# Sliding heads of the last two rows of an attention-and-MLP kernel: values as the stationary operand, exponentials as the moving one, row sums spread over 64 partitions

## The chip, the cores and the metric

The kernel runs on one core of a Trainium2 chip. The time is that of one execution on the device, in microseconds (us). The core's engines are named as in the profile: PE is TensorE (matmuls), PEld its weight loads, DVE is VectorE, ACT is ScalarE, POOL is GpSimd, and SP issues DMAs. PSUM is where matmuls write; it has eight banks.

## What is computed

An attention layer with 8 batch rows, 8 heads, 576 positions and head size 64, and behind it a two-layer perceptron. Heads 0 to 3 look at the last 32 positions ("sliding"), heads 4 to 7 at every fourth of the last 128 ("dilated").

```python
scores = scale * np.matmul(q, k.transpose(0, 1, 3, 2))
mask_plain = (rel >= 0) & (rel < 32)
mask_dil = (rel >= 0) & (rel < 128) & (rel % 4 == 0)
attn = np.exp(scores - max);  attn = attn / (sum(attn) + 1e-09)
attn_out = np.matmul(attn, v)
x = attn_out.transpose(0, 2, 1, 3).reshape(B * S, H * D)     # 4608 x 512
h = x @ w_in                                                 # 512 -> 2048
out = (np.maximum(h, 0) ** 2) @ w_out                        # 2048 -> 512
```

## The kernel before

**Layout.** The perceptron wants x with features on partitions: the tile xT has 128 partitions x 4 feature chunks x a ring of 4 x 576 tokens. Chunks 0 and 1 hold the sliding heads (two heads of 64 features each), chunks 2 and 3 the dilated ones. The first product (mm1_tile, matmul at L264) multiplies xT by w_in, ScalarE applies relu (L249), VectorE squares (L253) into g. The second product (mm2, L296) multiplies g by w_out, and store copies the result out. For the last two chunks of 512 tokens the second product has another form (seven_gen, matmuls at L401, sums on VectorE).

**Order.** The order of all instructions on each engine is written out by hand: a generator of perceptron steps stands in a list, and pump(n) takes n steps from it, two matmuls of 512 columns each. For rows 2 to 7 (the loop over b) the perceptron of the row before is pending; attention steps are issued with pump between them: 24 steps first, then the scores (attn_scores, four groups with 4 steps behind each), then the values (attn_values, ten places with 2 steps behind each), then the rest (pump(1000)). Behind row 7 come the two last chunks.

**Scores.** Scores come out transposed, keys on partitions and queries along the free dimension: 128 keys against blocks of 96 queries for the sliding heads (L560), of 72 for the dilated ones (L574). ScalarE takes the exponential into the tile AT (L547), and VectorE multiplies by the mask (L549).

**Values.** The value tile vp holds, for each block of 96 queries and each head, its 128 keys x (64 values and a column of ones). In av_sliding the exponentials are the stationary operand (128 keys x 128 columns) and vp the moving one (65 columns, L615): queries come out on partitions, with 64 values and the sum for each of four heads. normalize takes the reciprocal of the sums, 8 for each partition (L600), and multiplies (L601) into an fp16 tile x. x_sliding then turns that tile with six matmuls against the identity (L644), and ScalarE copies the outcome to xT (L650). The dilated heads go the same way (av_dilated L629, x_dilated L662 and L668). Per row there are three groups of av_sliding (two query blocks each), two of x_sliding, four of av_dilated and two of x_dilated.

**PSUM.** From row 1 on, the perceptron and the turned tiles (except row 1's) take banks 0 to 3 in turn, and all groups of scores and values take two pairs of banks in turn (pairs [2, 3]); so a group of values writes where the group before the last did, and has to wait until normalize has read that one.

**Set-up.** v_ones writes the ones of the value tiles on VectorE (L747 to L750), once for each of two copies of the tiles: at L775 in the start, at L842 before the first perceptron steps in a run. GpSimd casts the values in (L197, L201).

Of the kernel before, what the change touches and what calls it, by code (L numbers as in the profile page):

```python
# [8 lines left out]
FP16 = mybir.dt.float16  # L9
FP32 = mybir.dt.float32  # L10
I16 = mybir.dt.int16
ALU = mybir.AluOpType
ACTF = mybir.ActivationFunctionType
P = 128
# [3 lines left out]
def kernel(  # L18
# [9 lines left out]
    nc = tc.nc  # L28

    B, H, S, D = q.shape  # L30
# [5 lines left out]
    HH = H // 2  # L36
# [5 lines left out]
    HALF = S // 2  # L42
# [3 lines left out]
    QB = 96  # L46
    NB = S // QB
    PADP = P - QB
# [7 lines left out]
    const = ctx.enter_context(tc.tile_pool(name="const", bufs=1))  # L56
# [3 lines left out]
    xp = ctx.enter_context(tc.tile_pool(name="xp", bufs=4))  # L60
# [19 lines left out]
    def pair(dt=FP32):  # L80
        i = pairs[turn["pair"] % len(pairs)]
        turn["pair"] += 1
        b = PS[:, 2 * i : 2 * i + 2, :]
        return b if dt == FP32 else b.bitcast(dt)
# [3 lines left out]
    xT = const.tile([P, NDM, RING], FP16, name="xT")  # L88
# [18 lines left out]
    QKTp = [const.tile([P, 2, 2, PADP + S], FP16, name=f"QKTp{r}") for r in range(2)]  # L107
    QKTd = [const.tile([P, 2, 2, KPAD + S], FP16, name=f"QKTd{r}") for r in range(2)]
    AT = const.tile([P, 8, 640], FP16, name="AT")
    vp = [const.tile([P, NB, HH, D + 2], FP16, name=f"vp{r}") for r in range(2)]  # L110
    vd = [const.tile([P, 2, DIL, HH, D + 2], FP16, name=f"vd{r}") for r in range(2)]
    sv = stg.tile([P, NB, HH, D], FP32, name="sv")
    sd = stg.tile([P, 2, HH, DIL * D], FP32, name="sd")
# [109 lines left out]
    def in_token_order(b, n):  # L223
        o = natp.tile([P, 9, HH, D], FP16, name=f"o{b}", tag="o")
        nc.gpsimd.tensor_copy(o, n.rearrange("p h j d -> p j h d"))  # L225
        return o
# [259 lines left out]
    def pump(n):  # L486
        for _ in range(n):
            while pending:
                try:
                    next(pending[0])  # L490
                    break
                except StopIteration:
                    pending.pop(0)
# [3 lines left out]
    def pt(wide):  # L497
        return pair(FP16)[:, 0, :] if wide else bank(FP16)
# [97 lines left out]
    def normalize(b, what, pav, w):  # L596
        x = xp.tile([QB, 2, HH, D], FP16, name=f"x{b}_{what}", tag="x")
        rcp = xp.tile([QB, 2, HH], FP32, name=f"rcp{b}_{what}", tag="rcp")
        pv = pav[0:w, :, 0 : HH * (D + 2)].rearrange("p i (h d) -> p i h d", d=D + 2)
        nc.vector.reciprocal(rcp[0:w], pv[:, :, :, D])  # L600
        nc.vector.tensor_tensor(  # L601
            out=x[0:w],
            in0=pv[:, :, :, 0:D],
            in1=rcp[0:w].unsqueeze(3).to_broadcast([w, 2, HH, D]),
            op=ALU.mult,
        )
        return x

    def av_sliding(b, mp):
        pav = pair()  # L610
        for i in range(2):
            m = 2 * mp + i
            for h in range(HH):
                off = (h % 2) * 288 + (m % 3) * QB
                nc.tensor.matmul(  # L615
                    pav[:, i, h * (D + 2) : h * (D + 2) + D + 1],
                    AT[:, 2 * (h // 2) + m // 3, off : off + P],
                    vp[b % 2][:, m, h, 0 : D + 1],
                    start=True,
                    stop=True,  # L620
                )
        return normalize(b, f"p{mp}", pav, QB)

    def av_dilated(b, t, a):
        pav = pair()
        for e in range(2):
            for h in range(HH):
                off = e * 288 + h * QD
                nc.tensor.matmul(  # L629
                    pav[:, e, h * (D + 2) : h * (D + 2) + D + 1],  # L630
                    AT[:, 4 + 2 * a + t, off : off + P],
                    vd[b % 2][:, t, 2 * a + e, h, 0 : D + 1],
                    start=True,
                    stop=True,
                )
        return normalize(b, f"d{t}_{a}", pav, QD)

    def x_sliding(b, half, xs, wide):
        px = pt(wide)
        for m3 in range(3):  # L640
            m = 3 * half + m3
            x = xs[m // 2][:, m % 2].rearrange("p h d -> p (h d)")
            for c in range(2):
                nc.tensor.transpose(  # L644
                    px[:, 288 * c + QB * m3 : 288 * c + QB * (m3 + 1)],
                    x[:, P * c : P * (c + 1)],
                    ident[0:QB, 0:QB],
                )
        t0 = (b % 4) * S + 288 * half
        nc.scalar.copy(  # L650
            xT[:, 0:2, t0 : t0 + 288],
            px[:, 0:UW].rearrange("x (c t) -> x c t", c=2),
        )

    def x_dilated(b, t, xs, wide):
        py = pt(wide)
        for a in range(2):
            for e in range(2):
                x = xs[a][:, e].rearrange("p h d -> p (h d)")
                for c in range(2):  # L660
                    o = 288 * c + QD * (2 * a + e)
                    nc.tensor.transpose(  # L662
                        py[:, o : o + QD],
                        x[0:QD, P * c : P * (c + 1)],
                        ident[0:QD, 0:QD],
                    )
        t0 = (b % 4) * S + 288 * t
        nc.scalar.copy(  # L668
            xT[:, 2:4, t0 : t0 + 288].rearrange("x c (i r) -> x c i r", r=DIL),
            py[:, 0:UW].rearrange("x (c r i) -> x c i r", c=2, r=DIL),  # L670
        )
# [8 lines left out]

    def attn_values(b, gap, wide=False):
        xs = []
        for mp in range(3):
            xs.append(av_sliding(b, mp))
            pump(gap)
        x_sliding(b, 0, xs, wide)
        pump(gap)
        ys = [av_dilated(b, 0, 0)]
        pump(gap)
        x_sliding(b, 1, xs, wide)  # L690
        pump(gap)
        ys.append(av_dilated(b, 0, 1))
        pump(gap)
        zs = []
        for a in range(2):
            zs.append(av_dilated(b, 1, a))
            pump(gap)
        x_dilated(b, 0, ys, wide)
        pump(gap)
        x_dilated(b, 1, zs, wide)  # L700
# [43 lines left out]
        )  # L744

    def v_ones(r):
        nc.vector.memset(vp[r][:, :, :, D : D + 1], 1.0)  # L747
        nc.vector.memset(vp[r][0:PADP, 0, :, D : D + 1], 0.0)
        nc.vector.memset(vd[r][:, 1, :, :, D : D + 1], 1.0)
        nc.vector.tensor_scalar(  # L750
            out=vd[r][:, 0, :, :, D],
            in0=relf[:, 0:1].unsqueeze(2).to_broadcast([P, DIL, HH]),
            scalar1=-PADD + 0.5,
            scalar2=None,
            op0=ALU.is_lt,
        )
# [15 lines left out]
    for a in range(2):  # L772
        t_dilated_one(0, nd0, a, 1, tk[:, a, :])
        c_dilated_one(0, a, 1, tk[:, a, :], nc.vector)
    v_ones(0)  # L775
    for a in range(2):
        t_dilated_one(0, nd0, a, 0, tq[:, a, :])
# [49 lines left out]
    xs = [av_sliding(0, mp) for mp in range(2)]  # L827
    x_dilated(0, 0, ys, True)
    x_sliding(0, 0, xs, True)
    pairs[:] = [2, 3]  # L830
    pending.append(mm1_first_gen())
# [8 lines left out]
    x_sliding(0, 1, xs, True)  # L840
    k_pads(1)
    v_ones(1)  # L842
    ns1 = natp.tile([P, HH, 9 * D], FP16, name="ns1", tag="n")
    nd1 = natp.tile([P, 36 * D], FP16, name="nd1", tag="nd")
    for i, src in ((1, k), (0, q)):
        nc.gpsimd.dma_start(
            out=ns1[64 * i : 64 * (i + 1)],
# [19 lines left out]
    o = in_token_order(2, n)  # L867
# [16 lines left out]
    s_dilated(1, 1)  # L884
    pump(4)
    attn_values(1, 1, True)
    pump(1000)
    load_v(2)
# [3 lines left out]
    for b in range(2, B):  # L892
        pending.append(moe_gen(b - 1))
        if b + 1 < B:
            see(QKTp[b % 2][0:1, 0, 0, PADP : PADP + 1])
            n, dd = load_whole_sliding_qk(b + 1), keep_dilated_qk(b + 1)
            o = in_token_order(b + 1, n)
            transpose_dilated(b + 1, dd)
            transpose_sliding(b + 1, keep_sliding_qk(b + 1, o))
        cast_v(b)  # L900
        if b + 1 < B:
            load_v(b + 1)
        if b + 1 < B:
            pump(24)
        else:
            quarters()
            for name in ("T1", "T3", "T2", "T4"):
                for j in range(2):
                    pump(3)
                    sum_w_out(name, j)  # L910
        attn_scores(b, 4)
        attn_values(b, 2)
        pump(1000)
# [33 lines left out]
```

## Time and profile before

| | |
|---|---|
| median of 3 runs (314.5 to 316.2) | 314.87 us |
| the profiled execution | 315.87 us |
| its span, first to last instruction | 313.8 us |
| mean granted TensorE clock | 0.995 |
| busy: PE, DVE, ACT, POOL | 299.6, 181.7, 167.3, 78.0 us |
| values of row 6 | about 212.6 to 225.8 |
| values of row 7 | about 244.9 to 258.1 |

Times in the views count from the span's start. A line such as "L601 ... x24 | 16.5, 686 | 0.8" is a group of instructions: line, engine, operation, output and inputs, shape, count, then busy us, mean ns of one, and the idle time of the engine just before them. The chain is the work that ended last, followed back from the end to what released each step.

### The profile page before, as it was taken

What the parts mean: (1) busy time and instruction counts of PE and PEld (TensorE: products, weight loads), DVE (VectorE), ACT (ScalarE), POOL (GpSimd) and SP (SyncE); (2) the same over time, 40 slices, a digit from 0 to 9 for tenths busy, and PEclk for the clock granted to TensorE, in tenths of its full rate; (3) what the DMA queues carried; (4) which work ended last, traced back from release to release, by engine and by line L of the source; (5) the groups of instructions that cost most, each with busy time, mean ns of one, the idle gap of its engine ahead of it and who ended that gap; (6) DMA issues with size and microseconds to landing.
All of it is one profiled execution on the core that took longest, in us unless ns stands there. A gap on an engine that the chain in (4) does not pass through costs nothing.

```text
span 313.8 us, 6835 instructions
## 1 busy us (share of the span) xinstructions
PE 299.6 (96%) x2724; PEld 183.7 (59%) x2724; DVE 181.7 (58%) x402; ACT 167.3 (53%) x295; POOL 78.0 (25%) x120
## 2 busy tenths in 40 slices
PE   3978999999899999999999999999999999999995
PEld 3647955555455555555579655545554555686584
DVE  6445647736742795396524653475388534854764
ACT  2646856378336753677257724683368336604610
POOL 5483016403523633263340370032000000000000
PEclk9989999999999999999999999999999999999999
DMA  6999989599989999998968992992100110012012
GB/s 118 223 191 214 212 179 216 123 164 256 229 185 202 278 193 188 236 280 172 221 218 193 176 239 75 186 206 101 45 25 1 41 61 36 1 40 96 0 36 100
DMA packets 73951, 46.71 MB, mean 149 GB/s; under 512 B 54528, under 2 KB 68096, under 8 KB 73728
## 3 DMA queue, kind: packets, MB, share of 16 engines
q1 hardware_dynamic: 66384, 32.39, 43.2%
q0 software_dynamic: 7248, 13.63, 24.4%
q8 instruction: 21, 0.34, 0.4%
q10 hardware_dynamic: 288, 0.26, 0.2%
q14 instruction: 10, 0.08, 0.1%
HBM read 39.85 MB, written 16.52 MB: 180 GB/s over the span
## 4 chain that ended last, share of the span: by engine, by line
PE 88%; DMA 7%; POOL 2%; issue 1%; ACT 1%; DVE 0%; POOLq 0%
PE PS L264 39%; PE PS L296 30%; PE PS L401 8%; PE PS L629 3%; DMA wi<-in_moe_w_in_dram 3%; DMA sd<-in_v_dram 2%; DMA n<-in_q_dram 2%; PE PS L615 2%; PE PS L574 1%; PE PS L644 1%; PE PS L560 1%; PE PS L662 1%; ACT AT L547 0%; PE PS L504 0%; PE PS L528 0%
## 5 line engine op out<-in xcount | busy, mean ns | idle before, releaser
L264 PE MATMUL PS<-xT,wi 128*128 128x512 f16 (+3 forms) x704 | 130.3, 343 | 1.8 <-DMA wi<-in_moe_w_in_dram 1.1
L249 ACT ACTIVATE rt<-PS 128x512 f16<-128x512 f32 (+2 forms) x160 | 88.8, 556 | 44.6 <-PE PS L264 40.5
L296 PE MATMUL PS<-wo,g 128*128 128x512 f16 x448 | 112.5, 379 | 0.0
L253 DVE TENSOR_TENSOR g<-rt 128x512 f16<-128x512 f16 (+2 forms) x160 | 69.8, 443 | 72.1 <-ACT rt L249 71.5
L264 PEld LDWEIGHTS <-wi 128*128 128x128 f16 x704 | 78.4, 114 | 46.8 <-DMA wi<-in_moe_w_in_dram 1.2
L296 PEld LDWEIGHTS <-g 128*128 128x128 f16 x448 | 37.3, 97 | 31.4
L547 ACT ACTIVATE AT<-PS 128x576 f16<-128x576 f32 x64 | 38.3, 650 | 8.6 <-PE PS L574 5.7
L306 ACT COPY ot<-PS 128x512 f32<-128x512 f32 x28 | 16.4, 586 | 28.8 <-PE PS L296 28.8
L650 ACT COPY xT<-PS 128x576 f16<-128x576 f16 x16 | 10.2, 639 | 29.4 <-PE PS L644 29.4
L201 POOL CAST vd<-sd 128x512 f16<-128x512 f32 x32 | 20.5, 669 | 14.7 <-DMA sd<-in_v_dram 12.5
L197 POOL CAST vp<-sv 128x512 f16<-128x512 f32 x24 | 16.7, 710 | 27.1 <-DMA sv<-in_v_dram 27.1
L601 DVE TENSOR_TENSOR x_d<-PS,rcp_d 72x512 f16<-72x512 f32 x32 | 22.0, 686 | 1.1
L225 POOL COPY o<-n 128x2304 f16<-128x2304 f16 x6 | 12.6, 2107 | 27.8 <-DMA n<-in_q_dram 27.6
L549 DVE TENSOR_TENSOR AT<-AT,maskd 128x576 f16<-128x576 f16 x28 | 14.6, 539 | 7.0 <-ACT AT L547 5.6
L600 DVE RECIPROCAL rcp_d<-PS 72x8 f32<-72x8 f32 x32 | 6.5, 202 | 20.7 <-PE PS L629 19.6
L629 PEld LDWEIGHTS <-AT 128*128 128x128 f16 x256 | 12.8, 102 | 7.8 <-DVE x_d L601 0.8
L601 DVE TENSOR_TENSOR x_p<-PS,rcp_p 96x512 f16<-96x512 f32 x24 | 16.5, 686 | 0.8
L549 DVE TENSOR_TENSOR AT<-AT,maskp 128x576 f16<-128x576 f16 x28 | 14.3, 524 | 4.0 <-ACT AT L547 2.1
L668 ACT COPY xT<-PS 128x576 f16<-128x576 f16 x16 | 10.2, 640 | 8.8 <-PE PS L662 8.8
L629 PE MATMUL PS<-vd,AT 128*128 128x65 f16 x256 | 14.3, 200 | 0.0
L183 POOL COPY look<-QKTp 1x1 f16<-1x1 f16 x5 | 1.2, 239 | 49.3 <-DMA QKTp<-dp 49.3
L615 PEld LDWEIGHTS <-AT 128*128 128x128 f16 x192 | 9.2, 99 | 6.6 <-issue 1.2
(86 smaller groups left out, 207.9 us busy)
## 6 DMA issues: line engine op xcount, KB each, us to landing
out_dram<-ot SPq DMA_DIRECT2D x27, 256.0 KB, 2.8
sv<-in_v_dram SPq DMA_DIRECT2D x40, 128.0 KB, 4.6
sd<-in_v_dram SPq DMA_DIRECT2D x8, 512.0 KB, 11.4
dp<-o SPq DMA_DIRECT2D x12, 288.0 KB, 3.7
sd<-in_v_dram SPq DMA_DIRECT2D x8, 288.0 KB
wo<-in_moe_w_out_dram POOLq DMA_DIRECT2D x4, 512.0 KB, 13.6
out_dram<-c SPq DMA_DIRECT2D x14, 128.0 KB, 1.8
n<-in_k_dram POOLq DMA_DIRECT2D x6, 288.0 KB, 6.1
```

Source lines behind the costliest of these rows:

```text
L197: nc.gpsimd.tensor_copy(vp[b % 2][:, m : m + 2, :, 0:D], sv[:, m : m + 2, :, :])
L201: nc.gpsimd.tensor_copy(vd[b % 2][:, t, c : c + 2, :, 0:D], sd[:, t, :, D * c : D * (c + 2)].rearrange("p h (c d) -> p c h d", d=D),)
L249: nc.scalar.activation(rt[:, 0:w], ph[:, 0:w], ACTF.Relu)
L253: nc.vector.tensor_mul(g, rt[:, o : o + n], rt[:, o : o + n])
L264: nc.tensor.matmul(ph[:, a:b], w_in_of(dmk, ffc), xT[:, dmk, x : x + b - a], start=(dmk == 0 and a == 0), stop=(dmk == NDM - 1 and b == w),)
L296: nc.tensor.matmul(po, g[:, ffc, o + t * P : o + (t + 1) * P], w_out_of(ffc), start=(ffc == 0), stop=(ffc == NFF - 1),)
L306: nc.scalar.copy(ot, po)
L401: nc.tensor.matmul(po[t], lhs(j)[:, t * P : (t + 1) * P], rhs(j), start=j == 0, stop=j == HF - 1)
L547: nc.scalar.activation(AT[:, u, 0:UW], ps[:, :, 0 : UW // 2], ACTF.Exp, scale=scale)
L549: eng.tensor_mul(AT[:, u, 0:UW], AT[:, u, 0:UW], mask)
L601: nc.vector.tensor_tensor(out=x[0:w], in0=pv[:, :, :, 0:D], in1=rcp[0:w].unsqueeze(3).to_broadcast([w, 2, HH, D]), op=ALU.mult,)
L629: nc.tensor.matmul(pav[:, e, h * (D + 2) : h * (D + 2) + D + 1], AT[:, 4 + 2 * a + t, off : off + P], vd[b % 2][:, t, 2 * a + e, h, 0 : D ...
```

## The change

It touches rows 6 and 7 (b >= B - 2) and the sliding heads alone. The tile vp gets 128 columns for each head in place of 66: 64 values and 64 ones. v_ones fills all 64.

Row 7 (values_of_head): one head at a time. For each of six query blocks, one matmul with a stationary operand of 128 columns, which is the 64 values of the head and 64 ones (for odd heads the ones of the head before stand first), and the exponentials as the moving operand, 96 columns. Values come out with features on partitions and queries along the free dimension, and the other 64 partitions hold the sum of each query, 64 times over. VectorE takes the reciprocal of all these sums (64 partitions x 576) and multiplies the values by it straight into xT.

Row 6 (values_of_two): two heads and half of the queries at a time, in twelve matmuls of 64 stationary columns: values of two heads in one bank, one head on partitions 0 to 63 and one on 64 to 127, and their sums in the other bank. VectorE's reciprocal and product cover 128 partitions x 288.

So in these rows x is not turned, normalize is not used for the sliding heads, and ScalarE doesn't copy them; the four new groups come first, each with a pump behind it, and there are nine such places in place of ten. The dilated heads stay as they are.

```diff
-    vp = [const.tile([P, NB, HH, D + 2], FP16, name=f"vp{r}") for r in range(2)]
+    vp = [const.tile([P, NB, HH, 2 * D], FP16, name=f"vp{r}") for r in range(2)]
...
+    def spread_slots(b, m, h):
+        v_ = vp[b % 2][:, m].rearrange("p h x -> p (h x)")
+        o = 2 * D * h - (D if h % 2 else 0)
+        return v_[:, o : o + 2 * D]
+
+    def exps_of(h, m):
+        off = (h % 2) * 288 + (m % 3) * QB
+        return AT[:, 2 * (h // 2) + m // 3, off : off + QB]
+
+    def values_of_head(b, h):
+        ps = pair()
+        for m in range(NB):
+            o = QB * (m % 3)
+            nc.tensor.matmul(
+                ps[:, m // 3, o : o + QB], spread_slots(b, m, h), exps_of(h, m), start=True, stop=True
+            )
+        e = h % 2
+        mine, other = slice(64 * e, 64 * e + 64), slice(64 - 64 * e, 128 - 64 * e)
+        r = xp.tile([P, 2, HALF], FP32, name=f"r{b}_{h}", tag="r", bufs=1)
+        nc.vector.reciprocal(r[mine], ps[other, :, 0:HALF])
+        t0 = (b % 4) * S
+        nc.vector.tensor_tensor(
+            out=xT[mine, h // 2, t0 : t0 + S].rearrange("p (i t) -> p i t", i=2),
+            in0=ps[mine, :, 0:HALF],
+            in1=r[mine],
+            op=ALU.mult,
+        )
+
+    def values_of_two(b, hp, half):
+        ps = pair()
+        for m3 in range(3):
+            m = 3 * half + m3
+            for i in range(2):
+                for e in range(2):
+                    h = 2 * hp + e
+                    nc.tensor.matmul(
+                        ps[64 * e : 64 * e + 64, i, QB * m3 : QB * (m3 + 1)],
+                        vp[b % 2][:, m, h, D * i : D * (i + 1)],
+                        exps_of(h, m),
+                        start=True,
+                        stop=True,
+                    )
+        r = xp.tile([P, 2, HALF], FP32, name=f"r{b}_{hp}_{half}", tag="r", bufs=1)
+        nc.vector.reciprocal(r[:, 0, :], ps[:, 1, 0:HALF])
+        t0 = (b % 4) * S + HALF * half
+        nc.vector.tensor_tensor(
+            out=xT[:, hp, t0 : t0 + HALF], in0=ps[:, 0, 0:HALF], in1=r[:, 0, :], op=ALU.mult
+        )
...
     def attn_values(b, gap, wide=False):
         xs = []
-        for mp in range(3):
-            xs.append(av_sliding(b, mp))
+        spread = b >= B - 2
+        if spread:
+            for i in range(4):
+                if b == B - 1:
+                    values_of_head(b, i)
+                else:
+                    values_of_two(b, i % 2, i // 2)
+                pump(gap)
+        else:
+            for mp in range(3):
+                xs.append(av_sliding(b, mp))
+                pump(gap)
+            x_sliding(b, 0, xs, wide)
             pump(gap)
-        x_sliding(b, 0, xs, wide)
-        pump(gap)
         ys = [av_dilated(b, 0, 0)]
         pump(gap)
-        x_sliding(b, 1, xs, wide)
-        pump(gap)
+        if not spread:
+            x_sliding(b, 1, xs, wide)
+            pump(gap)
         ys.append(av_dilated(b, 0, 1))
...
     def v_ones(r):
-        nc.vector.memset(vp[r][:, :, :, D : D + 1], 1.0)
-        nc.vector.memset(vp[r][0:PADP, 0, :, D : D + 1], 0.0)
+        nc.vector.memset(vp[r][:, :, :, D : 2 * D], 1.0)
+        nc.vector.memset(vp[r][0:PADP, 0, :, D : 2 * D], 0.0)
```

## The prediction

> **What bounds the kernel now.** I read four views: the page's chain of work, the same chain in order of time, VectorE's timeline beside it, and VectorE's groups by form. The page's chain gives the span to TensorE:
>
> ```profile
> PE 88%; DMA 7%; POOL 2%; issue 1%; ACT 1%; DVE 0%; POOLq 0%
> ```
>
> In order of time, around the values of row 7 (columns: start, us on the chain, what):
>
> ```profile
> 244.93 0.25 PE PS L615 x8
> 245.19 0.86 PE PS L296 x4
> 246.05 0.26 PE PS L615 x8
> ...
> 248.29 0.26 PE PS L644 x6
> 248.54 0.86 PE PS L296 x4
> 249.41 0.25 PE PS L629 x8
> ```
>
> No idle piece stands between them: a group of attention matmuls (0.25 us), four matmuls of the second product (0.86 us), and so on through row 6 (212.6 to 225.8) and row 7 (244.9 to 258.1). An edit gains here only what it takes off TensorE, and anything that makes TensorE wait is lost in full, since the stages behind are as dense. VectorE in the same stretch (columns: start, duration, operation, in brackets idle before):
>
> ```profile
> 245.22 0.20 DVE L600 RECIPROCAL rcp_p<-PS 96x8 f32<-96x8 f32 x1 [0.53 <-PE PS L615]
> 245.46 0.69 DVE L601 TENSOR_TENSOR x_p<-PS,rcp_p 96x512 f16<-96x512 f32 x1
> 246.34 0.20 DVE L600 RECIPROCAL rcp_p<-PS 96x8 f32<-96x8 f32 x1 [0.19 <-PE PS L615]
> 246.58 0.69 DVE L601 TENSOR_TENSOR x_p<-PS,rcp_p 96x512 f16<-96x512 f32 x1
> ```
>
> It needs 0.20 + 0.04 + 0.69 = 0.93 us per group and is offered one each 1.12 us (245.22 to 246.34): 0.19 us are free. These groups write to only two PSUM pairs in turn (pairs [2, 3]), so group n+2 can't start before VectorE is through with group n. That is the wait that ends last if VectorE slows down.
>
> **Removed from TensorE, per row:** three sliding groups (3 x 0.25) and two groups of turning matmuls (2 x 0.26), 1.28 us. ScalarE loses two copies of 0.64 us; it idles up to 3.0 us between such copies in row 7, so that is worth nothing.
>
> **Added on TensorE, row 7:** 4 heads x 6 matmuls of 96 columns from full 128-row weights. L644 is six matmuls of 96 columns: 0.26 us. 4 x 0.26 = 1.04 us, so -0.24 us. **Row 6:** 4 groups of 12 matmuls of 96 columns with 64 weight columns, which the trace before doesn't show. Between 25 ns each (64x64 tiles of L504: 36 of 64 columns in 0.59 us, times 96/64) and 43 ns (L644, nothing overlapped): 1.18 to 2.06 us, -0.1 to +0.8. I take L560's rate, 12 of 96 columns in 0.36 us, as it is the nearest packed row: 4 x 0.36 = 1.44, +0.16 us. Both rows: -0.08 us.
>
> **Added on VectorE: the inverse over everything.** A reciprocal now takes 8 elements per partition; afterwards it takes 576 (row 7, four times) or 288 (row 6, four times). Everything hangs on what one more element costs, and no row shows a long reciprocal. The rows that split a duration into a fixed part and a slope:
>
> ```profile
> L601 DVE TENSOR_TENSOR x_p<-PS,rcp_p 96x512 f16<-96x512 f32 x24 | 16.5, 686 | 0.8
> L600 DVE RECIPROCAL rcp_p<-PS 96x8 f32<-96x8 f32 x24 | 4.8, 202 | 7.1 <-PE PS L615 7.1
> L193 DVE COPY QKTp<-PS 128x576 f16<-128x576 f16 x5 | 3.8, 758 | 4.8 <-PE PS L504 4.8
> L472 DVE TENSOR_TENSOR c<-PS,v 128x256 f32<-128x256 f32 x4 | 1.7, 424 | 1.3 <-PE PS L401 1.3
> L456 DVE TENSOR_TENSOR c<-PS,t 128x512 f32<-128x512 f32 x2 | 1.4, 692 | 0.7 <-PE PS L401 0.7
> L726 DVE CAST relf<-reli 128x96 f32<-128x96 int16 x1 | 0.2, 210 | 0.6 <-POOL reli L710 0.6
> ```
>
> L456 less L472: 268 ns for 256 elements, 1.047 ns each. Taking that slope off, the fixed part of an instruction that reads PSUM is 150 ns (L601), 155 (L193), 156 (L456, L472). The reciprocal reads the same PSUM tile as L601 and takes 203 (its median) for 8 elements, where 153 + 8 would be 161. The missing 42 ns are either fixed, or they belong to the elements. The ends: all fixed, so 1.047 ns each with 195 fixed; or the fixed part is only that of a one-element memset (59 ns, L721), and an element costs 18 ns. I take the fixed part of the rows nearest to it, 153, so (203 - 153) / 8 = **6.25 ns** per element (5.9 to 6.6 over these rows).
>
> Reciprocals: 576 elements 153 + 3600 = 3.75 us, 288 elements 153 + 1800 = 1.95. Products, at L601's fixed part and 1.047 ns: 0.76 and 0.46 us. With the 0.04 us between the two, a head of row 7 costs VectorE 4.55 us and a group of row 6 2.45, where TensorE would bring one each 1.12 and 1.22 (0.26 or 0.36, plus 0.86).
>
> **The wait.** Count from the first group's start. Row 7: VectorE starts at 0.46 (ScalarE's copy starts at 248.58 behind an equal group, six L644, that started at 248.12) and is through with four heads at 0.46 + 4 x 4.55 = 18.66. Dilated group 01 is the sixth on TensorE and takes the buffer of head 3: it can start at 18.71 (0.05 is L644's hand-over behind L601). Without waiting it would start at 4 x 1.12 + 1.11 = 5.59. Lost: **13.1 us**, in four waits of about 3.4 (before heads 2 and 3 and dilated 00 and 01). Behind it VectorE needs 0.93 per 1.11 again and catches up. Row 6: 0.55 + 4 x 2.45 + 0.05 = 10.40 against 4 x 1.22 + 1.11 = 5.99: **4.4 us**. Behind each waiting matmul stands all of TensorE, the second product too, though it has its own banks: the order is fixed and one pump fewer (9 for 10) only moves four matmuls behind the values. Here row 6's extra TensorE time comes off its wait.
>
> **The clock.** Each wait of row 7 leaves TensorE idle for 3.4 of 4.55 us. The trace has half speed at the start (columns: stretch, length, busy PE, PEld, DVE, ACT, POOL, granted clock, DMA share, GB/s):
>
> ```profile
> 20.00:22.00 2.00, 1.23 (x10) 0.88 (x11) 0.00 (x0) 0.44 (x2) 1.14 (x3) 0.68 1.25 216
> 22.00:23.00 1.00, 1.00 (x11) 0.72 (x9) 0.57 (x3) 0.36 (x1) 1.00 (x3) 0.50 1.15 205
> 24.00:25.00 1.00, 1.00 (x15) 0.89 (x14) 0.93 (x4) 0.41 (x1) 1.00 (x3) 0.93 1.09 207
> ```
>
> After 1.05 us idle before 20.77 and two shorter waits the clock is 0.50 for some 3.4 us of dense work, which cost 1.7 us; the waits of 0.7 us from 26 to 27.3 cost none. During the waits a slow clock is hidden; behind the last it costs 0 to 3.4 us (one window or two). I take one: +1.7.
>
> The Trainium skill, "TensorE: Matmul & The Clock Gate", Part 1, has an idle window of about 3.4 us halve the clock and as long a busy one restore it; the waits here come to the edge of that, so by the page it is 0 or about 1.7 us.
>
> **Ones.** Each call of v_ones fills 1536 elements for 24, and 256 for 4. Memset rows: 912 ns for 1024, 272 for 256, so 0.833 ns each: 1.34 us for 0.08, 0.27 for 0.06: +1.47 us. The first call ends at 9.45 for 7.98; the copies at 8.77 and 9.99 move by 0.7 and 0.2, under TensorE's bias matmuls (to 11.07) and its 0.53 us wait for a DMA at 12.1, and the first product waits 1.05 us for its weights. The second call falls in 1.70 us of idle VectorE before 28.50. Nothing; without cover 0.7 us at most each. The POOL casts have the same sizes and wait for nothing new.
>
> **Sum.** 13.1 + 4.4 - 0.1 = 17.4, plus 1.7 of clock: 19.1. The profiled execution took 315.87 (span 313.8): 335.0. It is 1.0 above the median of 314.87, so 334.0 there, 332.3 without the clock.
>
> **Rivals.** (a) The element is dearer: the one-input row L726 leaves 210 - 101 = 110 fixed, which makes 11.6 ns; halfway to mine 8.9. The wait grows by 4 x 568 + 4 x 280 ns = 3.39 us per ns, so +9.0: 341.3 without the clock, 350 at 11.6. For: one input, like the reciprocal; against: it doesn't read PSUM. The Trainium skill ("VectorE: DVE Perf Modes", Walkthrough, the fixed hardware budget) speaks against this change: reciprocal is an iterative divide with a repeat count of 8. Read as 8 cycles of the 0.96 GHz that its first page gives, an estimate of 8.3 ns, it would make 339.4; the row's 203 ns for 8 elements lies between that and mine.
> (b) Not slower: the 42 ns are fixed, and the element costs 1.047 ns. A reciprocal of 576 is 0.80, a head 1.59 us. Row 7 waits 0.46 + 4 x 1.59 + 0.05 - 5.59 = 1.3 us, row 6 (0.99 per 1.22) not at all: +1.2, 316.1, within 0.5%, about what a measurement of this kernel can tell from no change. It decides at a slope below 1.2 ns. Against: 42 ns unaccounted for.
> (c) The clock stays up: 332.3; or it drops in row 6 too: 336.
>
> **Chances.** Slope 5 to 7.5, with or without the clock: 0.60. (a): 0.25. (b): 0.10. Something else: 0.05. Faster by 0.5% needs 1.6 us, where TensorE can gain 0.34: 0.02. Low end 327 is a slope of 4.7 without the clock; high end 342 takes in 8.9; 350, 372 (18 ns) and (b) stay out.
>
> **To see afterwards:** reciprocals of 3.75 and 1.95 us; in row 7 four TensorE waits of about 3.4 us for VectorE's product, none from dilated 10 on; the granted clock behind the last; the memsets at 1.34 us with the first product still at 20.8. I am wrong if a reciprocal of 576 lasts under 1 us, or the wait stands elsewhere.

## The result, and the profile after

The changed kernel takes **335.47 us** (median of 4 runs, 335.24 to 335.65) where the kernel before took 315.38 (4 runs, 314.5 to 316.2): 1.064 times as long, 95% interval 1.060 to 1.067. The profiled execution took 335.41 us, with a span of 333.3.

The chain of work of the changed kernel, from its page:

```profile
PE 83%; DVE 11%; DMA 2%; ACT 1%; POOL 1%; issue 1%; DVEq 0%; POOLq 0%
```

VectorE had none of the chain before. Now the reciprocals and products of the two rows have 27.9 us of it, four times 3.77 + 0.76 in row 7 and four times 1.97 + 0.47 in row 6, beside which some of TensorE's own work lies. The chain in order of time shows row 7 (columns: start, us on the chain, what; lines of the code have moved, L298 is the second product, L631 the dilated values):

```profile
249.42 0.27 PE PS L655 x6
249.69 0.02 issue
249.71 3.77 DVE r L661
253.48 0.02 issue
253.50 0.76 DVE xT L663
...
268.26 0.62 PE PS L631 x8
268.88 1.71 PE PS L298 x4
270.58 0.44 PE PS L631 x8
271.02 1.53 PE PS L298 x4
272.55 0.26 PE PS L631 x8
```

From the first head on, the end is set by reciprocal, product, reciprocal, product, four times over, until at 268.26 the dilated group 01 gets its buffer. Behind it four second-product matmuls take 1.71 us, where they took 0.86 before: half speed, until about 272.5.

The new groups on VectorE (columns: busy us, mean ns of one, idle before):

```profile
L661 DVE RECIPROCAL r<-PS 64x576 f32<-64x576 f32 x4 | 15.0, 3755 | 0.8 <-PE PS L655 0.5
L686 DVE RECIPROCAL r<-PS 128x288 f32<-128x288 f32 x4 | 7.8, 1957 | 1.0 <-PE PS L678 0.7
L663 DVE TENSOR_TENSOR xT<-PS,r 64x576 f16<-64x576 f32 x4 | 3.0, 755 | 0.1
L688 DVE TENSOR_TENSOR xT<-PS,r 128x288 f16<-128x288 f32 x4 | 1.8, 457 | 0.1
L811 DVE MEMSET vp<- 128x1536 f16 x2 | 2.7, 1338 | 0.5 <-issue 0.5
```

TensorE's waits (in total us, times, longest), of which the trace before has none for VectorE in these rows:

```profile
PE PS L655 <- DVE xT L663: 5.8, 2, 3.1
PE PS L631 <- DVE xT L663: 4.6, 2, 2.3
PE PS L631 <- DVE xT L688: 2.4, 2, 1.3
PE PS L678 <- DVE xT L688: 1.4, 2, 1.1
```

In each row two waits stand before the third and fourth sliding group and two before the dilated groups 00 and 01. They add up to 14.2 us. Much of the rest of the loss is work at half clock behind the last wait of each row (1.9 and 1.5 us, by the experiments below). Between the waits of row 7 it only makes them shorter.

The start of the kernel scatters: row 6's values begin at 212.41 in the trace before, at 210.56 after, at 214.62 in that of e6 below. So the experiments are best read by the **stretch** of a row: from its first group of values to the first matmul of the next mm1, which holds the same second-product work in each kernel (added matmuls apart). Before, both rows have 13.18 us; after, row 6 has 19.51 and row 7 28.23, 21.4 us more in all. The span grew by 19.5, as that trace reached row 6 earlier by 1.9.

### The profile page after: what moved, and what is told of

The parts are those of the page before. It is cut to its first block, busy times and chain, and to the rows that moved or that the text cites. A ratio compares the mean times of both kernels' runs of the same rounds, so it can differ in the third digit from the quotient of the medians.

```text
span 333.3 us, 6841 instructions
## 1 busy us (share of the span) xinstructions
PE 306.3 (92%) x2724; PEld 185.0 (55%) x2724; DVE 205.9 (62%) x406; ACT 164.5 (49%) x291; POOL 77.3 (23%) x120
## 4 chain that ended last, share of the span: by engine, by line
PE 83%; DVE 11%; DMA 2%; ACT 1%; POOL 1%; issue 1%; DVEq 0%; POOLq 0%
PE PS L266 38%; PE PS L298 27%; PE PS L403 7%; DVE r L661 5%; PE PS L631 3%; DVE r L686 2%; DMA ns<-in_q_dram 2%; PE PS L562 2%; PE PS L576 1%; PE PS L716 1%; PE PS L617 1%; PE PS L698 1%; DVE AT L551 1%; DVE xT L663 1%; DVE x_p L603 1%
## 5 line engine op out<-in xcount | busy, mean ns | idle before, releaser
L298 PE MATMUL PS<-wo,g 128*128 128x512 f16 x448 | 117.1, 392 | 0.0
L255 DVE TENSOR_TENSOR g<-rt 128x512 f16<-128x512 f16 (+2 forms) x160 | 68.8, 434 | 72.3 <-ACT rt L251 71.5
L298 PEld LDWEIGHTS <-g 128*128 128x128 f16 x448 | 38.3, 100 | 33.9 <-issue 3.2
L631 PEld LDWEIGHTS <-AT 128*128 128x128 f16 x256 | 13.5, 108 | 17.4 <-DVE xT L663 6.4
L631 PE MATMUL PS<-vd,AT 128*128 128x65 f16 x256 | 15.3, 208 | 7.0 <-DVE xT L663 4.6
L704 ACT COPY xT<-PS 128x576 f16<-128x576 f16 x12 | 7.7, 638 | 20.7 <-PE PS L698 20.7
L661 DVE RECIPROCAL r<-PS 64x576 f32<-64x576 f32 x4 | 15.0, 3755 | 0.8 <-PE PS L655 0.5
L722 ACT COPY xT<-PS 128x576 f16<-128x576 f16 x16 | 10.2, 640 | 6.8 <-PE PS L716 6.8
L603 DVE TENSOR_TENSOR x_p<-PS,rcp_p 96x512 f16<-96x512 f32 x18 | 12.4, 687 | 0.6
```

The costliest lines, as they stand in the source:

```text
L255: nc.vector.tensor_mul(g, rt[:, o : o + n], rt[:, o : o + n])
L298: nc.tensor.matmul(po, g[:, ffc, o + t * P : o + (t + 1) * P], w_out_of(ffc), start=(ffc == 0), stop=(ffc == NFF - 1),)
L603: nc.vector.tensor_tensor(out=x[0:w], in0=pv[:, :, :, 0:D], in1=rcp[0:w].unsqueeze(3).to_broadcast([w, 2, HH, D]), op=ALU.mult,)
L631: nc.tensor.matmul(pav[:, e, h * (D + 2) : h * (D + 2) + D + 1], AT[:, 4 + 2 * a + t, off : off + P], vd[b % 2][:, t, 2 * a + e, h, 0 : D ...
L661: nc.vector.reciprocal(r[mine], ps[other, :, 0:HALF])
```

## The experiments

The theory: an element of a reciprocal costs VectorE about 6 ns, a group of values then occupies it for 2.5 or 4.6 us, and since two PSUM pairs take turns TensorE stands still at its pace. Rivals: the groups, partitions or ones of the new form cost it; two buffers are too few; one of the rows drags the other. All ratios are to the kernel before, run on the same chip.

**One row at a time (e1, e2).**

```diff
-        spread = b >= B - 2
+        spread = b == B - 1      # e1;  b == B - 2 in e2
```

> The change in row 7 alone; row 6 keeps the old form. Theory (each inverse of 576 elements lasts 3.75 us on VectorE, two PSUM pairs, TensorE waits for the product): row 7 costs on its own what its stretch grew by in the trace of the change, some 15 us: 329.5 to 330.5. Rival (the two rows hang together: what is late in row 6 makes row 7 worse, or the wide ones cost throughout): below 327 or not the difference that row 6 alone leaves.

> The change in row 6 alone; row 7 keeps the old form. Theory: some 6 us (4.5 of waiting, 1.5 of half clock behind it): 320.8 to 321.8, and with row 7 alone it adds up to the whole change. Rival: the 64-column matmuls, not the inverse, are what row 6 pays for: then TensorE shows no waits for VectorE's product there.

Row 7 alone: 331.04 us (328.66 to 332.94, 0.5 above what was expected), ratio 1.049 (1.043 to 1.056); stretch 28.73. Row 6 alone: 319.65, ratio 1.013 (1.010 to 1.017); stretch 17.99. The two medians are 15.7 and 4.3 us above before (315.33), together 20.0 where the change has 20.1. The runs of row 7 alone scatter over 4 us, so the traces say more: the last wait ends 19.00 us behind the first group in row 7 and 10.65 in row 6, in these traces as in that of the change. The waits of one row don't hang on the other's. Row 6 alone came out 1.2 us below the low end that was expected, and its trace says why. Behind its last wait (chain in order of time):

```profile
222.05 0.43 PE PS L631 x8
222.48 0.86 PE PS L298 x4
```

Here the four matmuls run at full speed; in the profiled execution of the whole change the same place has

```profile
221.21 0.62 PE PS L631 x8
221.82 1.71 PE PS L298 x4
```

This form has a stretch of 18.0 us in e2, e4, e5 and in row 7 of e9 below, and 19.5 or 19.6 in the trace of the change and in row 6 of e9: the clock falls there in some executions. The wait itself is 4.25 us (17.99 less the 13.74 that the row takes without waiting, below).

**A copy for the inverse (e3).**

```diff
-        nc.vector.reciprocal(r[mine], ps[other, :, 0:HALF])
+        nc.vector.tensor_copy(r[mine], ps[other, :, 0:HALF])
```

(and the same in row 6)

> Leaves the inverse out: a copy of the same elements stands where the reciprocal stands, in both rows. Same groups, buffers, order and ones. Theory (the price of an element of the reciprocal): a copy of 576 from PSUM is 0.76 us (as L193 before), a head 1.64 us for 1.12 offered, row 7 waits about 1.5 us, row 6 not at all: 316.5 to 317.5. Rival (the new groups, the halves of the partitions or the wide ones themselves cost the time): above 325.

316.83 us, ratio 1.004 (1.001 to 1.008). VectorE in row 7:

```profile
243.47 0.76 DVE L661 COPY r<-PS 64x576 f32<-64x576 f32 x1 [0.53 <-PE PS L655]
244.27 0.75 DVE L663 TENSOR_TENSOR xT<-PS,r 64x576 f16<-64x576 f32 x1
245.12 0.75 DVE L661 COPY r<-PS 64x576 f32<-64x576 f32 x1
```

The same bytes, halves, buffers and order: 0.76 us for 3.76, and 18.6 of the 20.1 us are gone. The rival that blames the form itself is out. Row 7's stretch is still 14.34 us for 13.18 before: a head takes 1.65 us where one is offered each 1.12.

**Half the inverse in row 7 (e4).**

```diff
-        nc.vector.reciprocal(r[mine], ps[other, :, 0:HALF])
+        nc.vector.reciprocal(r[mine, 0], ps[other, 0, 0:HALF])
...
-            in1=r[mine],
+            in1=r[mine, 0:1, :].to_broadcast([64, 2, HALF]),
```

> Row 7 leaves the inverse of half its queries out: reciprocal over 288 of 576 elements, used for both halves; row 6 as in the change. Theory: 1.96 for 3.75 us, a head 2.85 for 4.65 us, the wait of row 7 falls from 13.4 to 6.3: 328 to 329. Rival (a fixed price for each such instruction): 335.

327.26 us, ratio 1.038 (1.034 to 1.042), 0.7 below what was expected. The reciprocal of 288 elements lasts 1.96 us on 64 partitions too. Row 7's stretch is 21.07, of which some 1.8 is the clock: the four matmuls behind its last wait are slow here too. The price goes with the number of elements, not of instructions.

**Three pairs of banks (e5).** nbanks is the number of banks that the perceptron takes in turn.

```diff
+        if b == B - 1:
+            nbanks[0] = 2
+            pairs[:] = [1, 2, 3]
         attn_values(b, 2)
         pump(1000)
+        nbanks[0] = 4
```

> In the values of row 7 three PSUM pairs take turns in place of two, and the perceptron has two banks in place of four there. Theory (VectorE's rate sets the end, a buffer only moves which group waits): dilated group 10 waits in place of 01, one step of 1.1 us later: 1.1 to 1.4 us off, 334.0 to 334.5. Rival (the buffers are what binds; one more hides the inverse): the four waits of row 7 shrink by several us, below 330.

336.21 us, ratio 1.066 (1.060 to 1.072): nothing gained, not even the 1.1. TensorE's waits (this copy's lines are one further):

```profile
PE PS L632 <- DVE xT L664: 8.0, 3, 3.4
PE PS L656 <- DVE xT L664: 1.5, 1, 1.5
PE PS L267 <- ACT ot L309: 0.7, 1, 0.7
PE PS L299 <- ACT ot L309: 0.4, 1, 0.4
```

Now three dilated groups wait in place of two, as expected, the last of them until 267.83, 19.03 us behind the first head; with two pairs the last wait ended 19.00 behind it. So the step was won, and lost again to a price of the edit: with two banks TensorE waits 1.1 us for ScalarE to copy results of the second product out, 0.4 in that product (L299) and 0.7 ahead of the next first product (L267). The buffers are not what binds; that one more gives 1.1 us wasn't shown.

**Matmuls in the waits (e6).**

```diff
+    def keep_busy(n):
+        po = bank()
+        for j in range(n):
+            nc.tensor.matmul(po, wo[0][:, 0, 0:P], wo[1][:, 0, :], start=True, stop=True)
```

called ahead of the four waiting groups of each row, n = 10 in row 7 and 4 in row 6.

> Adds work: 10 matmuls of 512 columns that nothing uses ahead of each waiting group in row 7, 4 in row 6 (8 places, 56 matmuls, 12.1 us of TensorE at full clock). Theory (part of the loss is the clock that falls in the idle stretches and is still low behind the last wait): the added matmuls lie in the waits, the granted clock stays at 1.00, and 1.5 to 3.5 us come back: 332 to 334. Rival (the clock costs nothing, or the matmuls don't fit in the waits): 335.5 or above.

333.64 us, ratio 1.055 (1.049 to 1.061); the medians give 1.8 us back, less than the scatter of these four runs (331.97 to 336.07) can settle. The granted clock is clear: over the whole execution 0.990 to 0.995 in the four runs, for 0.964 in all four of the change. So is row 7's stretch: 26.34 for 28.23, with 8.6 us of work added there. Row 6 has 18.00 for 19.51, but 18.0 came without added work as well (e2, e4, e5), so that the added matmuls won it isn't shown. TensorE in row 7 (columns: start, duration, operation; idle before):

```profile
262.62 2.32 PE L738 MATMUL PS<-wo,wo 128*128 128x512 f16 x10
266.15 0.43 PE L631 MATMUL PS<-vd,AT 128*128 128x65 f16 x8 [1.21 <-DVE xT L663]
266.42 1.02 PE L298 MATMUL PS<-wo,g 128*128 128x512 f16 x4
```

And windows of each kernel, the change first; in the second trace row 7 starts 2.5 us later, so its last wait ends at 270.80 and not at 268.26 (columns: stretch, length, busy PE, PEld, DVE, ACT, POOL, granted clock, DMA share, GB/s):

```profile
256.00:260.00 4.00, 1.04 (x8) 0.73 (x8) 3.86 (x3) 0.00 (x0) 0.00 (x0) 0.50 0.00 0
268.00:272.00 4.00, 3.74 (x23) 1.92 (x24) 2.78 (x7) 0.00 (x0) 0.00 (x0) 0.50 0.00 0
```

```profile
256.00:260.00 4.00, 3.50 (x22) 1.69 (x21) 3.86 (x3) 0.00 (x0) 0.00 (x0) 1.00 0.00 0
268.00:272.00 4.00, 2.80 (x23) 1.24 (x22) 3.87 (x6) 0.00 (x0) 0.00 (x0) 1.00 0.00 0
272.00:276.00 4.00, 4.00 (x48) 2.34 (x47) 2.23 (x5) 1.38 (x3) 0.00 (x0) 1.00 0.06 23
```

With TensorE kept busy the clock stays at 1.00, and the row ends 1.9 us sooner although its last wait ends 19.00 us behind the first head, as in the change: that much was the clock, 13.4 us (26.34 less 12.92, below) the wait.

**The inverse on ScalarE (e7).**

```diff
-        nc.vector.reciprocal(r[mine], ps[other, :, 0:HALF])
+        nc.scalar.activation(l[mine], ps[other, :, 0:HALF], ACTF.Ln)
+        nc.scalar.activation(r[mine], l[mine], ACTF.Exp, scale=-1.0)
```

(and the same in row 6; l is a new tile for the logarithms, and r has two buffers for one)

> The inverse is taken on ScalarE as exp(-ln(sum)), two activations of the same elements in place of VectorE's reciprocal, in both rows. Theory (only the element's price on VectorE matters): 0.65 us each, a buffer held 2.7 us for two heads, row 7 waits about 1.1 us: 316 to 317.5. Rival (ScalarE pays for the change between functions): each pair shows an extra load of a table before it, and the time is above 320.

340.82 us, ratio 1.079 (1.074 to 1.084): the rival holds. ScalarE in row 7:

```profile
256.33 1.28 ACT L662 ACT_TABLE_LOAD   x1
257.62 0.65 ACT L662 ACTIVATE l<-PS 64x576 f32<-64x576 f32 x1
258.29 1.28 ACT L663 ACT_TABLE_LOAD   x1
259.58 0.68 ACT L663 ACTIVATE r<-l 64x576 f32<-64x576 f32 x1
```

Each change between logarithm and exponential loads a table, 1.28 us, and a head takes 3.9 us of ScalarE. The loads are as long for a group of row 6, whose stretch is 24.47 for 19.51 in the change; row 7 has 27.64 for 28.23. The activations themselves are as short as expected. Whether both functions can go without a load between them wasn't tried.

**The ones alone (e8).**

```diff
-        spread = b >= B - 2
+        spread = False
```

> The wide value tile and its 64 ones alone: no row uses the new form. Theory: the memsets of 1.34 us lie in idle time of VectorE: 314.9 to 315.9, no change. Rival (the ones delay the start or the first products): 316.5 and a later first product.

315.71 us (10 runs), ratio 1.000 (0.997 to 1.003). The ones cost nothing that can be measured.

**Two heads at a time in row 7 too (e9).**

```diff
-                if b == B - 1:
-                    values_of_head(b, i)
-                else:
-                    values_of_two(b, i % 2, i // 2)
+                values_of_two(b, i % 2, i // 2)
```

> Row 7 takes row 6's form as well: two heads at a time, 128 partitions x 288. The sums, the groups and the pumps are as many; only the reciprocal is half as long, as it uses all partitions. Theory (the price is per element of one partition, whatever stands on the other partitions): a group 2.55 for 4.65 us, row 7's stretch falls from 28.2 to 18.1, or 19.6 if the clock falls: 325 to 327.5. Rival (the price is for the data, 64 x 576 being as much as 128 x 288): 335.

325.34 us, ratio 1.027 (1.019 to 1.035); row 7's stretch is 18.00 for 28.23. VectorE's group in both rows:

```profile
L686 DVE RECIPROCAL r<-PS 128x288 f32<-128x288 f32 x8 | 15.7, 1958 | 1.7 <-PE PS L678 1.1
```

As many sums, on twice the partitions, in half the time. Of the 15.0 us that the change adds to row 7's stretch, 10.2 (clock included) are gone once the reciprocal uses all 128 partitions in place of 64.

**The reciprocal by itself (e10).** The kernel before with nine instructions behind its end, two that fill s32 (SBUF, fp32) and pp (PSUM) from the fp16 weights w16, and these:

```diff
+        nc.vector.reciprocal(o32, pp[:, 0, :])
+        nc.vector.reciprocal(o32, s32)
...
+            nc.vector.reciprocal(o16, w16)
+        nc.vector.reciprocal(o32[:, 0:128], pp[:, 0, 0:128])
+        nc.vector.reciprocal(o32[:, 0:8], pp[:, 0, 0:8])
+        nc.vector.reciprocal(o32[0:1, :], s32[0:1, :])
+        nc.vector.tensor_copy(o32, pp[:, 0, :])
```

> The kernel before, with a row of reciprocals and copies on VectorE behind its end (some 17 us more, nothing uses their results): from PSUM 512, 128 and 8 elements of 128 partitions, from SBUF 512 in fp32, 512 in fp16, and 512 on one partition, and a copy of 512 from PSUM. Theory (6.25 ns per element of one partition, 153 ns fixed): 3.35, 0.95, 0.20, 3.35, 3.35, 3.35 and 0.69 us. Rivals: the slow read is PSUM's (then SBUF's is under 1 us), or fp32's (then fp16's is half or less), or it is for the partitions (then one partition is quick).

```profile
310.78 3.36 DVE L681 RECIPROCAL o<-PS 128x512 f32<-128x512 f32 x1
314.18 3.35 DVE L682 RECIPROCAL o<-s 128x512 f32<-128x512 f32 x1
317.44 3.29 DVE L684 RECIPROCAL o<-wo 128x512 f16<-128x512 f16 x1
320.66 0.90 DVE L685 RECIPROCAL o<-PS 128x128 f32<-128x128 f32 x1
321.58 0.21 DVE L686 RECIPROCAL o<-PS 128x8 f32<-128x8 f32 x1
321.83 3.34 DVE L687 RECIPROCAL o<-s 1x512 f32<-1x512 f32 x1
325.20 0.69 DVE L688 COPY o<-PS 128x512 f32<-128x512 f32 x1
```

The one run took 329.19 us. 512 elements last 3.3 us from PSUM or SBUF, in fp32 or fp16, on 128 partitions or on one; the copy of as many 0.69. All three rivals are out. 512 and 8 elements came within 0.01 us of the forecast (0.06 for fp16); 128 took 0.90 for 0.95, and why isn't shown.

**No inverse at all (e11).** VectorE copies the values to xT, with neither reciprocal nor product.

```diff
-        nc.vector.reciprocal(r[mine], ps[other, :, 0:HALF])
...
-            in0=ps[mine, :, 0:HALF],
-            in1=r[mine],
-            op=ALU.mult,
+        nc.vector.tensor_copy(
+            xT[mine, h // 2, t0 : t0 + S].rearrange("p (i t) -> p i t", i=2), ps[mine, :, 0:HALF]
+        )
```

(and the same in row 6)

> Leaves the inverse and the product out: VectorE only copies the values out of PSUM, in both rows. It bounds what the new form could give if the inverse were free. Theory: no waits of TensorE; row 7 takes its 0.24 us less, row 6 its 0.3 us more (twelve 64-column matmuls took 0.40 us in the trace of the change): 315.0 to 316.0, no change from before. Rival (the new form saves TensorE more than its matmuls say): 313.5 or less.

314.83 us (12 runs), ratio 0.998 (0.996 to 1.001): no change. The stretches are the form's bare TensorE time: row 7 12.92 us, row 6 13.74. Chain in order of time, row 6 (L673), then row 7 (L655):

```profile
211.23 0.38 PE PS L673 x12
211.60 0.97 PE PS L298 x4
212.57 0.38 PE PS L673 x12
```

```profile
244.24 0.26 PE PS L655 x6
244.50 0.86 PE PS L298 x4
245.36 0.26 PE PS L655 x6
```

Row 7 saves 0.23 to 0.26 us; row 6 loses 0.56 to 0.59, as twelve matmuls of 64 columns take 0.38 and the four between two such groups 0.97 for 0.86. The chain goes by ends, which are modelled. By the starts in TensorE's timeline the loss lies ahead of a 64-column group: behind the last such group, where one of 128 columns comes next, the four take 0.88. So even a free inverse leaves nothing to gain here, and no version of this form that beats the kernel before was found. By the stretches, a free inverse would bring 0.25 us in a row of row 7's form; that row by itself wasn't run so.

## Why the prediction was right, step by step

- **The price of an element.** Forecast 3.75 and 1.95 us, measured 3.755 and 1.957. The step that carried everything was to put the 50 ns between the short reciprocal and the fixed part of the rows nearest to it on the elements. It came out: 8, 288, 512 and 576 elements (203, 1957, 3358 and 3755 ns, e10 for the third) lie within 5 ns of 153 + 6.25 for each element, and 128 elements 58 below it. Rivals (a), 8.9 ns, and (b), 1.05 ns, are refuted by the same rows. The Trainium skill's page "VectorE: DVE Perf Modes" has the reciprocal as an iterative divide, which a price of six times a product's for each element fits. Its repeat count of 8, read as 8 cycles, made an estimate of 8.3 ns, and the rows decide for 6.25.
- **The wait.** Forecast 13.1 and 4.4 us. Measured without the clock's part: row 7 26.34 - 12.92 = 13.4 (e6 against e11), row 6 17.99 - 13.74 = 4.25 (e2 against e11). A head takes 4.65 us for the 4.55 of the sum, as the next reciprocal starts 0.10 behind the product (253.50 + 0.75 to 254.36); between four heads that is three times 0.1, the 0.3 that is missing. A group of row 6 has the same, 2.55 for 2.45, so its last wait ends 10.65 us behind the first group for the 10.40 forecast. That row 6's wait is still below the forecast is a second miss that sets off the first: without waiting dilated group 01 would have started at 6.41 (e11), not at 5.99.
- **What waits.** Forecast: before sliding groups 3 and 4 and dilated 00 and 01, none later. So it is. In row 7 they are 2.65, 3.10, 2.30 and 2.32 us long and not about 3.4: ahead of the first TensorE still has two groups to do, and behind it the work between them runs partly or wholly at half clock. e5 shows that the pairs choose which group waits and VectorE's rate how long.
- **The clock.** Forecast 1.7 behind row 7, 0 in row 6, with row 6 as rival (c). Row 7: 1.9 by e6, and 2.4 in e1 (28.73 for 26.34). One window was a choice between bounds of 0 and 3.4, and that it came so near is partly luck. Row 6: 1.5 in the profiled execution and 1.6 in row 6 of e9, 0 in e2, e4, e5 and row 7 of e9. So the second half of rival (c), a clock that drops in row 6 too, holds for the profiled execution. Why the clock falls there only at times wasn't tried; the four idle pieces of 0.2 to 1.3 us are the same in all. Row 6's idle pieces, 1.3 us at most, and the one of 2.65 us ahead of the fall in row 7 (0.90 granted in 252 to 256 us) are shorter than the window of about 3.4 us that the page "TensorE: Matmul & The Clock Gate" gives, so the page's single idle stretch is not what decides; e6 shows that filling part of the waits is enough.
- **TensorE's own time.** Row 7 forecast -0.24, measured -0.23 (12.92 for the 13.15 of e8). Row 6 forecast +0.16, measured +0.59: the groups took 0.38 for 0.36, and the four matmuls ahead of the next 64-column group 0.1 us more, which no row before showed. In the change most of that lay in row 6's wait.
- **The ones.** Forecast 1.34 us for each memset, measured 1.338; the small one took 0.17 for 0.27, as it went as 128 elements of uint32 (L812). The first product was to start at 20.8 still; in the trace of the change it starts at 19.88. No cost (e8).
- **The sum.** Forecast 19.1 us on the profiled execution's own terms. The terms as measured: 13.4 + 4.25 + 0.36 + 1.9 = 19.9, and 1.5 more where row 6's clock falls, 21.4. That is what the two stretches grew by in the profiled execution. It came within 0.4 us of the 335.0 forecast for it partly by luck: it reached row 6 1.9 us earlier than the trace before, which set off the 1.5 that the forecast had put at nothing. The medians differ by 20.1.

## What to carry to other kernels

A short instruction's duration hides its price per element behind the fixed part: before spreading an operation over more elements, take the fixed part off with rows of the same engine and source, and multiply what is left. On the chain, compare the rate at which groups are offered with the rate at which their reader frees buffers; one more buffer only moved the wait (e5). Where the price is for each element of a partition, use all the partitions (e9). An idle stretch on TensorE can cost again behind itself, by a clock that has fallen.

## What the runs showed of the hardware

- A reciprocal on VectorE costs 6.25 ns for each element of a partition ((3755 - 203) ns / 568 in the change), six times the 1.047 ns of a product. It is the same from PSUM and SBUF, in fp32 and fp16, on 128 partitions and on one (3.29 to 3.36 us for 512 elements in e10).
- Four second-product matmuls between two groups of 64-column matmuls take 0.97 us, between two of 128 columns 0.86 (e11). By the starts the 0.1 us lies ahead of the 64-column group: its weight loads start with its first matmul (both at 212.50), where those of row 7's groups start 0.22 us ahead of it (244.98 and 245.20). What holds them isn't shown.
- Waits of 1.1 to 1.3 us with 1.4 us of work between them halved the granted clock in some executions of the same code, and not in others (row 6: 0.63 on average in 220 to 224 us in the change, 1.00 in e2).
- Changing between logarithm and exponential on ScalarE cost 1.28 us each time (e7, 16 loads).
